# Filler products on TensorE around the first two attention units, and one copy moved from VectorE to ScalarE

## The chip, the cores and the metric

The kernel runs on one core of one Trainium2 chip. A core has a matrix engine (TensorE, PE in the profile, with its weight loads as PEld), three engines for elementwise work (VectorE or DVE, ScalarE or ACT, GpSimd or POOL), a queue that mostly issues transfers (SyncE, SP), and 16 DMA engines. The metric is the device time of one execution in microseconds; lower is better. Five runs of the kernel before gave a median of 304.19 us (303.46 to 305.06).

## The reference

Inputs q, k and v are float32 of 8 batches x 8 heads x 576 positions x 64. Attention is limited to a symmetric window of 32 positions, and a two-layer network with a sigmoid-gated activation follows on the 4608 tokens:

```python
scores = scale * np.matmul(q, k.transpose(0, 1, 3, 2))
mask = np.abs(pos[:, None] - pos[None, :]) <= window          # window = 32
scores = np.where(mask, scores, -1e9)
attn = softmax(scores)
x = (attn @ v).transpose(0, 2, 1, 3).reshape(4608, 512)
h = x @ w_in                                                  # 512 -> 2048
g = h * sigmoid(1.702 * h)
out = g @ w_out                                               # 2048 -> 512
```

## The kernel before

The 4608 tokens are cut into 36 attention units of 128 queries, each with two blocks of 64 queries and the 128 keys around each block. Two units make a tile of 256 tokens for the two layers, 18 tiles in all. The order of the instructions on each engine is the order in which the program calls them; nothing reorders it. A buffer (a tile of SBUF or a bank of PSUM) is taken from a ring of a fixed length, and the first instruction that writes it waits for the last reader or writer of what lay there before. PSUM has eight banks in four rings: two "h", one "o", four "a" and one "t" (`bank`).

The change is in `head`, the part ahead of the loop over windows. Its calls, in order, and what each puts on which engine:

- Loads. The q and k of the first 320 tokens (span "A") for four heads come by the SP and ACT queues; the rest (other heads of A, v of units 0 to 2, span "B" with the next 256 tokens, v of unit 3 and half of 4, four parts of w_in, then w_out and later spans) is issued by POOL, in that order.
- `keep_busy(n, kind)`, line 424: n products of a zero tile with itself, 128x256, into a bank of ring `kind`. Nobody reads them.
- `keys_T` and `queries_T` (lines 163 and 166): TensorE transposes keys or queries of a pair of heads into a bank; a copy on the engine given as the last argument (`cast`, line 106) moves them to kT or qT. For span B the rings are "htho" for keys and "hoth" for queries, one letter for each of the four pairs.
- `blind(u)`, line 232: two "mask products" of 128x512 that write large negative numbers into the two score banks of unit u where a key lies outside the window. The scores of units 0 to 3 are then added on top (`scores`, line 250), so that their exponentials (line 256, ACT, four for two units) need no mask afterwards.
- `odd_v(m, eng)`, lines 151 and 152: two copies of 64x528 make vo, the v of unit m moved by 64 tokens, for the second block of queries: the upper half of ve of m, and the lower half of ve of m+1.
- `values(u, kinds)`, line 279: 32 small products of the exponentials with ve and vo, into two banks of the rings named.
- `norm(u)`, lines 290 and 291: DVE takes the reciprocal of the sums and multiplies, once for each half of the heads; x results.
- `x_T(u, kind, eng)`, line 306: TensorE transposes x in two pairs, one for each half, and `eng` copies the result to xT.
- `layer1(t, d)`, line 319: a group of eight products with w_in into an "h" bank, and the activation g on ACT (line 321). ACT loads a table when it goes from exponentials to g. The third group needs the bank of the first, so it waits for the first g.

In `head`, scores of units 0 and 1 are followed by vo, values, x and transposes of unit 0, then of unit 1, then by mask products of unit 2, the transposes of span B, mask products of unit 3, scores of units 2 and 3, and then by layer 1 of the first tile with the values of units 2 and 3 in between. After that, TensorE has layer 1 and layer 2 (lines 331 and 381) to do without a break.

Of the kernel before, what the change touches and what calls it, by code (L numbers as in the profile page):

```python
# [23 lines left out]
NV = 8  # L24
# [4 lines left out]
class _Kernel:  # L29
# [117 lines left out]
    def odd_v(self, m, eng):  # L147

        vo = self.vo[m % NV]
        nxt = self.v_first if m == self.NU - 1 else self.ve[(m + 1) % NV][0:64]  # L150
        eng.tensor_copy(vo[64:128], self.ve[m % NV][64:128])
        eng.tensor_copy(vo[0:64], nxt)


    def heads_T(self, c, i, hp, kind):
# [271 lines left out]
    def head(self):  # L427

        nc, dve, act, pool = self.nc, self.nc.vector, self.nc.scalar, self.nc.gpsimd
        for hp in range(2):  # L430
            self.load_raw("k", hp, nc.sync)
            self.load_raw("q", hp, act)
        self.setup()
        for c in "kq":
            self.load_heads("A", c, (4, 8))
        self.setup_neg()
        for m in range(3):
            self.load_v(m)
        for c in "kq":
            self.load_heads("B", c)  # L440
        self.load_v(3)
        self.load_v(4, 0)
        for c in range(4):
            self.load_w_in(c)
        self.odd_v(2, pool)
        self.odd_v(3, pool)
        for c in (0, 2):
            self.load_w_out(c)
        self.setup_mask()
        self.cut_mask()  # L450
        for c in "kq":
            self.load_heads(1, c)
        self.load_w_out(1)
        self.load_v(4, 1)
        for m in range(5, 7):
            self.load_v(m)
        self.load_w_out(3)
        self.load_v(7)
        for c in "kq":
            self.load_heads(2, c)  # L460
        self.keep_busy(16)
        for hp in range(2):
            self.pair_heads("k", "A", hp, dve, self.stage["k", "raw", hp])
            self.pair_heads("q", "A", hp, act, self.stage["q", "raw", hp])
        for hp in range(4):
            self.keys_T("A", hp, "ht"[hp % 2], dve)
            self.queries_T("A", hp, "ho"[hp % 2], act)
            if hp < 2:
                self.blind(hp)
        self.scores(0)  # L470
        self.scores(1)
        self.odd_v(0, dve)
        self.keep_busy(5, "h")
        self.values(0, "hh")
        self.norm(0)
        self.odd_v(1, dve)
        self.x_T(0, "t", act)
        self.values(1, "oa")
        self.norm(1)
        self.x_T(1, "a", act)  # L480
        self.blind(2)
        for hp in range(4):
            self.keys_T("B", hp, "htho"[hp], dve)
            self.queries_T("B", hp, "hoth"[hp], act)
        self.blind(3)
        self.scores(2)
        self.scores(3)
        self.layer1(0, 0)
        self.values(2)
        self.norm(2)  # L490
        self.layer1(0, 1)
        self.values(3)
        self.norm(3)
        self.x_T(2, "t")
        self.layer1(0, 2)
        self.x_T(3, "o")
        self.layer1(0, 3)
        for d in range(4):
            self.layer1(1, d)
        dve.tensor_copy(self.v_first, self.ve[0][0:64])  # L500
        dve.tensor_copy(self.k_first, self.kT[:, :, 0:64])
        self.queries_wrap(0)
        for n in range(4):
            self.w_sums(n, 0)
        for c in "kq":
            for hp in range(4):
                self.pair_heads(c, 1, hp, dve)
        for t, d in ((0, 4), (0, 5), (1, 4), (1, 5), (0, 6), (0, 7), (1, 6), (1, 7)):
            self.layer1(t, d)
        l2 = [(lambda c=c, u=u: self.layer2(u, c, "hhot"[u], (dve, act)[u % 2])) for c in range(4) for u in range(4)]  # L510

        def run(n):
            for _ in range(n):
                l2.pop(0)()

        run(4)
        for hp in range(4):
            self.keys_T(1, hp, "a", dve)
            self.queries_T(1, hp, "a", act)
            run(1)  # L520
        self.scores(4)
        self.scores(5)
        for m in range(4, 7):
            self.odd_v(m, dve)
        self.band(4)
        run(3)
        self.band(5)
        run(1)
        self.values(4)
        self.norm(4)  # L530
        self.scores(6)
        run(1)
        self.gelu_table()
        self.values(5)
        self.norm(5)
        self.band(6)
        run(1)
        self.x_T(4, "a")
        run(1)
        self.x_T(5, "a", act)  # L540
        run(1)
        for c in "kq":
            for hp in range(4):
                self.pair_heads(c, 2, hp, pool)
        self.load_v(8)
        self.load_v(9)
        self.load_v(10)
        for c in "kq":
            self.load_heads(3, c)
        self.layer1(2, 0)  # L550
        self.values(6)
        self.norm(6)
        for n in range(2):
            self.w_sums(n, 1)
        for d in range(1, 3):
            self.layer1(2, d)
        self.x_T(6, "a")
        self.layer1(2, 3)
        for hp in range(4):
            self.keys_T(2, hp, "t", dve)  # L560
            if hp in (1, 2):
                self.w_sums(hp + 1, 1)
            self.queries_T(2, hp, "o", act)
            self.layer1(2, 4 + hp)
        for m in (7, 8, 9):
            self.odd_v(m, dve)
        for m in (11, 12, 13):
            self.load_v(m)
        for c in "kq":
            self.load_heads(4, c)  # L570
# [230 lines left out]
```

## Time and profile before

| what | value |
| --- | --- |
| median of five runs | 304.19 us (303.46 to 305.06) |
| the profiled execution's own time | 303.33 us |
| its span in the profile | 301.6 us |
| PE busy in the span | 293.6 us (97%) |
| DVE, ACT, POOL busy | 198.0, 197.0, 74.5 us |
| PE's share of the chain that ended last | 92% |
| line 319 (layer 1) PE busy | 135.2 us, 1152 products of 274 ns |
| mean granted clock of PE | 0.989 |

The span is the time from the first to the last instruction that the profile shows; what lies around it is the difference to the execution's own time. Busy shares are given for 40 equal slices of 7.54 us. PEclk is the clock that TensorE was granted, in tenths of full speed. A product's duration includes its way through the engine, so products in a row overlap, and the distance of their starts is less than the duration. The chain that ended last is followed back from the last instruction, at each step to what released it. A wait for several things is put down to the one that came last.

### The profile page before, as it was taken

Reading aid. Unit: us, or ns where it says so; the run is one execution under the profiler, and the core shown is the slowest. Engines: PE = TensorE matmul, PEld = TensorE weight load, DVE = VectorE, ACT = ScalarE, POOL = GpSimd, SP = SyncE. Lnnn points to the kernel's source line nnn. Section 1 sums busy time; section 2 is a strip of 40 time slices with the busy share of each in tenths; the row PEclk is TensorE's granted clock in tenths of the full one; section 3 lists DMA queues with packets and bytes.
Section 4 is the critical chain, followed back from the end, with each engine's and each line's share of the span. In section 5 each row is a group of like instructions: output and inputs, shape, how many; then the busy total and the mean of one; then the engine's idle time right before and its main releaser. Section 6 shows DMA issues by size and latency. Waiting matters only on the chain.

```text
span 301.6 us, 9776 instructions
## 1 busy us (share of the span) xinstructions
PE 293.6 (97%) x4165; PEld 244.1 (81%) x4165; DVE 198.0 (66%) x602; ACT 197.0 (65%) x331; POOL 74.5 (25%) x114
## 2 busy tenths in 40 slices
PE   7699999999999999999999999999999999999995
PEld 4469764866888888888888888888888888888884
DVE  3633558679795958595859585958595767684353
ACT  4576547685785858585858585859595848575330
POOL 8884516957131203320222020201000000000000
PEclk9959999999999999999999999999999999999999
DMA  9999996999999991999099909590933030303012
GB/s 145 163 206 205 197 187 117 180 181 202 195 73 160 178 136 11 161 184 138 7 163 186 141 3 141 74 139 4 139 72 107 3 108 2 104 4 104 2 70 70
DMA packets 92202, 35.16 MB, mean 117 GB/s; under 512 B 64512, under 2 KB 87808, under 8 KB 92160
## 3 DMA queue, kind: packets, MB, share of 16 engines
q0 software_dynamic: 60320, 18.16, 60.7%
q1 hardware_dynamic: 31392, 16.00, 24.2%
q8 instruction: 32, 0.52, 0.7%
q10 hardware_dynamic: 448, 0.39, 0.5%
q14 instruction: 10, 0.08, 0.1%
HBM read 36.96 MB, written 9.44 MB: 154 GB/s over the span
## 4 chain that ended last, share of the span: by engine, by line
PE 92%; DVE 4%; DMA 1%; ACT 1%; issue 0%; SPq 0%; DVEq 0%
PE h_ps L319 42%; PE o_ps L381 30%; PE o_ps L331 7%; PE pv L279 4%; PE sc L250 4%; PE tp L163 2%; DMA k_raw<-in_k_dram 1%; PE tp L689 1%; PE tp L166 1%; PE sc L232 1%; PE tp L306 1%; DVE x L291 1%; DVE p L268 0%; DVE kT L106 0%; DVE kc L106 0%; DVE o_sb L399 0%
## 5 line engine op out<-in xcount | busy, mean ns | idle before, releaser
L319 PE MATMUL h_ps<-xT,w_in_sb 128*128 128x256 bf16 x1152 | 135.2, 274 | 0.0
L321 ACT ACTIVATE g<-h_ps 128x512 f16<-128x512 f32 x144 | 85.9, 597 | 69.7 <-PE h_ps L319 67.6
L319 PEld LDWEIGHTS <-w_in_sb 128*128 128x128 bf16 x1152 | 112.4, 98 | 13.8
L144 POOL DMA_DIRECT2D ve<-in_v_dram x40 | 34.2, 860 | 122.1 <-DVE rec L290 86.5
L381 PEld LDWEIGHTS <-gs 128*128 128x128 f16 x480 | 45.8, 98 | 5.8
L381 PE MATMUL o_ps<-w_sum,gs 128*128 128x256 f16 x360 | 44.3, 273 | 0.0
L256 ACT ACTIVATE p<-sc 128x512 bf16<-128x512 f32 x72 | 37.2, 603 | 3.5 <-PE sc L250 3.4
L358 DVE TENSOR_TENSOR gs<-g 128x512 f16<-128x512 f16 x30 | 12.6, 421 | 38.7 <-ACT g L321 38.6
L381 PEld LDWEIGHTS <-g 128*128 128x128 f16 x360 | 34.2, 98 | 4.5 <-ACT g L321 0.2
L291 DVE TENSOR_TENSOR x<-pv,rec 128x256 bf16<-128x256 f32 x72 | 30.5, 424 | 2.5
L381 PE MATMUL o_ps<-w_out_sb,g 128*128 128x256 f16 x240 | 29.1, 273 | 0.0
L106 DVE COPY part<-o_ps 128x256 f32<-128x256 f32 x45 | 19.0, 423 | 12.3 <-PE o_ps L381 11.4
L399 DVE TENSOR_TENSOR o_sb<-o_ps,part 128x256 f32<-128x256 f32 x45 | 19.0, 422 | 12.1 <-PE o_ps L381 11.5
L268 DVE TENSOR_TENSOR p<-p,mask 128x512 bf16<-128x512 bf16 x64 | 24.7, 424 | 1.3 <-ACT p L256 1.1
L331 PE MATMUL o_ps<-w_out_sb,g 128*128 128x512 f16 x96 | 23.2, 380 | 0.0
L256 ACT ACT_TABLE_LOAD x15 | 19.2, 1283 | 0.3
L418 ACT ACT_TABLE_LOAD x15 | 19.2, 1283 | 0.3
L290 DVE RECIPROCAL rec<-pv 128x4 f32<-128x4 f32 x72 | 12.5, 174 | 8.2 <-PE pv L279 8.2
L106 DVE COPY kT<-tp 128x512 bf16<-128x512 bf16 (+3 forms) x24 | 12.3, 531 | 8.2 <-PE tp L163 6.1
L279 PEld LDWEIGHTS <-p 128*64 128x64 bf16 x576 | 12.0, 111 | 6.5 <-DVE p L268 1.9
L250 PEld LDWEIGHTS <-kT 64*64 64x64 bf16 x1152 | 12.0, 110 | 5.1 <-issue 4.8
L279 PE MATMUL pv<-ve,p 128*64 128x65 bf16 x288 | 15.7, 198 | 0.4 <-DVE p L268 0.3
(71 smaller groups left out, 287.0 us busy)
## 6 DMA issues: line engine op xcount, KB each, us to landing
out_dram<-o_sb SPq DMA_DIRECT2D x34, 256.0 KB, 2.8
ve<-in_v_dram POOLq DMA_DIRECT2D x32, 128.0 KB, 5.0
w_in_sb<-in_moe_w_in_dram POOLq DMA_DIRECT2D x4, 512.0 KB, 11.2
w_out_sb<-in_moe_w_out_dram POOLq DMA_DIRECT2D x4, 512.0 KB, 12.2
ks<-in_k_dram POOLq DMA_DIRECT2D x2, 448.0 KB, 10.3
qs<-in_q_dram POOLq DMA_DIRECT2D x2, 448.0 KB, 12.7
ks<-in_k_dram POOLq DMA_DIRECT2D x3, 256.0 KB, 7.7
qs<-in_q_dram POOLq DMA_DIRECT2D x3, 256.0 KB, 8.4
```

The lines of the kernel that those rows point to most:

```text
L106: (eng.copy if eng is self.nc.scalar else eng.tensor_copy)(out, in_)
L144: self.nc.gpsimd.dma_start(self.ve[m % NV][off:off + n, :, :self.D], self.v[b, :, s:s + n, :].rearrange("h s d -> s h d"))
L250: nc.tensor.matmul(sc[eo][lo:lo + 64, 2 * hp + blk, :], self.kT[r, hp, at:at + 64], self.qT[r, JT * hp:JT * hp + JT, q0:q0 + 16], start=(s ...
L256: nc.scalar.activation(p[:, eo].rearrange("k h (s j) -> k h s j", j=JT), sc[eo].rearrange("k h (j s) -> k h s j", j=JT), AF.Exp, scale=sel ...
L268: self.nc.vector.tensor_mul(pv, pv, msk.to_broadcast([128, 4, 2, SQ]))
L279: nc.tensor.matmul(acc[half][blk * 64:blk * 64 + 64, hh, :], p[:, h % 2, h // 2 * 2 + blk, :], vt[:, h, :D + 1], start=(hh == 0), stop=(hh ...
L291: nc.vector.tensor_mul(x[:, hs, :], acc[half][:, :, :D], rec[:, hs, :].to_broadcast([128, 4, D]))
L319: nc.tensor.matmul(hps[:, i, :], self.w_in_sb[:, kr, ff * 128:(ff + 1) * 128], self.xT[t][:, kr, :], start=(i == 0 and kr == 0), stop=(i = ...
L321: nc.scalar.activation(self.g[t][:, ffs[0]:ffs[1] + 1:ffs[1] - ffs[0], :], hps, AF.Gelu_apprx_sigmoid)
L331: nc.tensor.matmul(o_ps, self.g[t][:, ff, s * 128:(s + 1) * 128], self.w_out_sb[:, ff, :], start=(ff == 0), stop=(ff == self.NFF - 1))
L381: nc.tensor.matmul(self.part[t, key], x, y, start=(first and k == 0), stop=(k == 7), skip_group_check=True)
L418: self.nc.scalar.activation(self.spark, self.spark, AF.Gelu_apprx_sigmoid)
```

## The change

In `odd_v` the two copies go through `cast`, which takes ScalarE's copy or another engine's, so that ScalarE can be given the work. In `head`:

- the vo copies of unit 1 go from DVE, where they came after the norm of unit 0, to ACT, where they come after the exponentials of units 0 and 1;
- six unread products into "o" come after the values of unit 0, two more into "o" after the transposes of x of unit 0, eight into "a" after the values of unit 1, and two into "h" ahead of the transposes of span B;
- the mask products of unit 3 come right after those of unit 2, before the transposes of span B instead of after them.

On TensorE these are 18 more products; no load or store is added or moved.

```diff
-        eng.tensor_copy(vo[64:128], self.ve[m % NV][64:128])
-        eng.tensor_copy(vo[0:64], nxt)
+        self.cast(eng, vo[64:128], self.ve[m % NV][64:128])
+        self.cast(eng, vo[0:64], nxt)
...
         self.odd_v(0, dve)
+        self.odd_v(1, act)
         self.keep_busy(5, "h")
         self.values(0, "hh")
         self.norm(0)
-        self.odd_v(1, dve)
+        self.keep_busy(6, "o")
         self.x_T(0, "t", act)
+        self.keep_busy(2, "o")
         self.values(1, "oa")
         self.norm(1)
+        self.keep_busy(8, "a")
         self.x_T(1, "a", act)
         self.blind(2)
+        self.blind(3)
+        self.keep_busy(2, "h")
         for hp in range(4):
             self.keys_T("B", hp, "htho"[hp], dve)
             self.queries_T("B", hp, "hoth"[hp], act)
-        self.blind(3)
         self.scores(2)
         self.scores(3)
```

## The prediction

> **What bounds the kernel now.** I began with the busy shares in 40 slices:
>
> ```profile
> PE   7699999999999999999999999999999999999995
> PEclk9959999999999999999999999999999999999999
> ```
>
> TensorE (PE) is full from slice 4 on, so the end comes earlier only if dense work begins earlier. One stretch is odd: in the third slice (15.1 to 22.6 us) PE had half its clock. I located it with windows of 0.1 us (edges at 15.10 and 21.92) and cut the stage at these edges; the columns are PE, weight loads, DVE, ACT, POOL, clock, DMA share and GB/s:
>
> ```profile
> 8.27:11.69 3.42, 2.39 (x84) 1.59 (x73) 2.60 (x8) 2.40 (x6) 3.42 (x6) 1.00 1.65 152
> 11.69:15.10 3.41, 2.11 (x34) 1.08 (x36) 1.87 (x7) 1.17 (x2) 2.01 (x3) 1.00 1.73 181
> 15.10:18.51 3.41, 3.32 (x100) 2.33 (x102) 1.64 (x4) 1.49 (x4) 2.71 (x5) 0.50 1.25 206
> 18.51:21.92 3.41, 3.41 (x67) 2.37 (x58) 0.64 (x3) 3.26 (x5) 3.06 (x12) 0.50 1.24 207
> ```
>
> The half clock follows PE's emptiest stretch. Next, the chain that ended last, within these stages (start, us, what):
>
> ```profile
> 12.05 0.38 DVE vo L152
> 12.43 0.04 issue
> 12.47 0.31 PE pv L279 x7
> ...
> 13.56 0.43 DVE x L291
> ...
> 15.06 0.65 PE tp L166 x16
> ...
> 16.20 0.85 PE tp L166 x15
> 17.05 0.97 PE sc L232 x2
> 18.02 1.00 PE sc L250 x41
> 19.02 1.82 PE h_ps L319 x8
> 20.84 0.58 PE pv L279 x12
> 21.42 1.24 PE h_ps L319 x8
> 22.66 0.38 PE pv L279 x16
> 23.04 0.33 PE tp L306 x4
> 23.37 0.87 PE h_ps L319 x8
> ```
>
> Up to 14 us the chain goes through DVE; from 16.2 it is PE alone, slow: eight products of line 319 take 1.82 us at 19.02 and 0.87 at 23.37. At 15.06 PE also waited for a transfer, in the waits of this stage:
>
> ```profile
> PEld L166 <- DMA qs<-in_q_dram: 0.2, 1, 0.2
> ```
>
> Last, ACT close behind PE in the timeline:
>
> ```profile
> 18.64 2.07 ACT L256 ACTIVATE p<-sc 128x512 bf16<-128x512 f32 x4 [1.18 <-PE sc L250]
> 20.73 1.28 ACT L321 ACT_TABLE_LOAD   x1
> 22.02 1.28 ACT L321 ACTIVATE g<-h_ps 128x512 f16<-128x512 f32 x2
> ```
>
> Its first g ends at 22.62 and frees the bank that the third layer-1 group needs; that group ran at 23.37. So ACT has 0.7 us in hand: a faster PE gains 0.7 us here and then meets ACT, unless the exponentials begin earlier too.
>
> **What the Trainium skill says.** "TensorE: Matmul & The Clock Gate", "What's actually happening": after an idle window of some 3.4 us TensorE gets half its clock, a busy window gives it back, and the windows run freely of the kernel's start. The trace agrees: 15.10 to 21.92 is 6.82 us, two such windows. The same page, "Part 4: PE-mode transpose", says that transposes do not count as busy for this in the same way. The trace speaks for it: in 15.10:18.51 PE was busy 3.32 of 3.41 us, 1.86 of it line 166's transposes, and the clock stayed at half. "ScalarE: Activation LUTs", "What ACT_TABLE_LOAD costs", gives 1283 ns for the load; the trace has the same.
>
> **The change part by part.** Sums are against the profiled execution, 303.33 us (span 301.6, 1.73 around it), assuming full clock throughout; then I ask whether it holds.
>
> Price of an unread product: line 424's five take 0.72 us with a mean of 275 ns each, so their starts are (0.72-0.275)/4 = 0.11 apart.
>
> 1. Six after the values of unit 0: 6 x 0.11 = 0.66, from 10.34 to 11.00. PE waited for x until 11.12 there, so they are hidden.
>
> 2. Two after the first transposes of x: 11.78 to 12.00. The values of unit 1 use the same bank and so wait for the end of the second, 11.89 + 0.275 = 12.17. Before they waited for DVE's vo until 12.47; hidden.
>
> 3. Both vo copies of unit 1 leave DVE (0.38 each, ended 12.43) for ACT, free from 11.02, when its exponentials end. No row shows such a copy on ACT: between 0.45 (one of its two 128x256 copies took 0.40) and 0.65 (POOL took 0.64); I take 0.6, by ACT's 128x512 copy of 0.59. They end at 12.25: 0.18 us earlier. The low price gives 11.95, but then step 2's 12.17 decides; the high one 12.35. Behind them on ACT waits the first xT copy, at 11.99 before and now 12.3 to 12.9. Its reader, line 319, comes at 18.5 or later.
>
> 4. Values at 12.29 instead of 12.47. From them to the end of the second x was 13.99-12.47 = 1.52, so 13.81. The eight products run from about 12.55 to 13.43. They delay the first pair of transposes (x ready at 13.27) by 0.15, but not the second: 13.86 instead of 14.04.
>
> 5. Mask products of unit 2: 13.98 to 14.41. Those of unit 3 now come here. The first runs at 14.41. The second reuses the bank of the transposed x, so it needs ACT's copy of it, which began 0.33 after the second pair: 14.19 + 0.59 = 14.78. That is a new wait, 0.2 us, with the whole of PE's queue behind it. It runs 14.82 to 15.04, then two junk products to 15.26. The transposes of line 166 begin there, against 14.69 for keys and 15.06 for queries: 0.2 us later than the transfer would allow.
>
> 6. 64 transposes at full clock: about 0.15 per eight (7.34 to 7.79 has three such steps), paced by four DVE copies of 0.42 and four ACT copies of 0.40, because banks are reused. Keys' last copy ends at 17.44, queries' at 17.68; before 17.30 and 17.46. So 0.22 later.
>
> 7. The mask products of unit 3, 0.97 on the chain at half clock, are gone from between transposes and scores. In the A stage the exponential began 0.36 after the last qT copy (8.61 to 8.97). So it begins at 17.68 + 0.36 = 18.04, not 18.64: 0.60 earlier.
>
> 8. ACT: 18.04 + 2.07 + 0.02 + 1.28 + 0.01 + 0.60 = 22.02. PE: w_in's first transfer, issued at 10.03, takes 8.5 (shortest of the four), so the first layer-1 group runs 18.57 to 19.44, values to 19.82, the second group to 20.69; unit 3's exponentials end at 20.11, so values to 21.07, transposes to 21.40. Then PE waits for ACT's bank: the third group starts at 22.06 instead of 23.37.
>
> The gain is 1.3 us. It stays, because PE is full afterwards. The next limits: qs of span 1 lands before DVE's 36.70, its first copy ends at 36.99, PE reads it at 39.35, 2.3 in hand. The last v of that stage, issued at 34.87 and 9.9 on its way, lands at 44.8; DVE used it at 45.80, so up to 0.3 us moves into DVE's queue, ahead of masks whose values have over 1 us in hand. At 303.33 this is 302.0; at the median, 304.19, it is **302.9**.
>
> Does the clock hold? In 11.69:15.10 a full array is given eight junk products after the values, two at their start, and two more mask products, about 1.3 us on top of 2.11, all in gaps: it should hold at 15.10. The next window is weaker: 0.22 of junk, 0.7 of scores, and transposes. If these count little, it is no fuller than the window that lost the clock.
>
> **The rivals.**
>
> *The clock falls at 18.51 instead.* For it: the half clock survived 15.10:18.51 although PE was busy. Against it: 4.86:8.27, also mostly transposes and masks, kept the clock. Then PE has 18.57 to 20.35, values to 20.95, the second group to 22.4 (full clock again at 21.92), values and transposes to 23.05: the third group 0.32 earlier, 303.9. If the clock falls at 15.10 after all, so that the change doesn't do what it says, removing the masks from before the scores leaves about 0.4: 303.8. One answer.
>
> *The median has less to give.* The windows run freely, and this profile may have caught a dear position. With the half clock ending 1 us earlier in before, the second group runs at full clock and the third would start near 22.9: gain 0.7 to 0.8, 303.45.
>
> *Slower.* The clock falls at 18.51 and stays low for two windows, to 25.3. Both groups then cost 1.8, the third begins at 23.6 and takes 1.75 to 25.35, against 24.24: 1.1 us lost, 305.3. It decides once the half clock lasts beyond about 24. Against it: at half clock, the same groups brought the clock back at 21.92.
>
> **How the numbers follow.** Full clock throughout 0.58 (302.9, own range 302.3 to 303.3); falls all the same 0.20 (303.8 to 303.9); less to give 0.15 (303.45); slower 0.07 (305.3). About 0.3%, 0.9 us, is what a measurement of this kernel can tell from none; 303.28 is the bound. Faster 0.58, the two middle cases within 0.3%: 0.35, slower 0.07. ACT's price moves the sum by 0.1 either way, the clock's position in before by 0.6 downward, so the range is 302.2 to 304.1.
>
> **What would show it.** Right: clock 1.00 from 15 to 25 us; vo of unit 1 on ACT ending near 12.25; the second mask product of unit 3 waiting for ACT near 14.8; the first exponential of unit 2 near 18.0; the third layer-1 group near 22.1, waiting for ACT. Wrong: a 0.50 in any slice there, the line-166 transposes beginning after 15.6, or a new wait in 34 to 46 us.

## The result

The changed kernel takes 304.11 us at the median (28 executions, 303.25 to 307.52), the kernel before 304.19 (47 executions). The ratio, which weighs all executions and not the medians alone, is 1.0015, 95% interval 0.9999 to 1.003: no change that can be told from none. Forecast were 302.9 us and a gain; the median lies 0.01 us beyond the upper end of the range, 304.1. The profiled execution took 303.66 us (span 302.0).

The executions are of two kinds. Each lists the mean clock that TensorE was granted. In 14 of 28 it was 0.998 or more, and their median is 303.58 us; in the other 14 it was 0.984 to 0.995, and their median is 305.20. The kernel before, in the comparisons below, had 0.983 to 0.989 in nearly every execution, which is two or three windows of half clock (two of 3.41 us each lower the mean over the span by 0.011).

The profiled execution is of the first kind. Its busy shares, as shown of before:

```profile
PE   8869999999999999999999999999999999999995
PEclk9999999999999999999999999999999999999999
```

The half clock is gone. The same stretches of time as before (PE, weight loads, DVE, ACT, POOL, clock, DMA share and GB/s) show what came in its place:

```profile
8.27:11.69 3.42, 2.89 (x93) 2.11 (x81) 1.76 (x7) 3.05 (x7) 3.42 (x5) 1.00 1.65 143
11.69:15.10 3.41, 3.03 (x37) 1.98 (x36) 1.46 (x5) 1.80 (x4) 2.23 (x4) 1.00 1.73 173
15.10:18.51 3.41, 3.09 (x133) 2.15 (x131) 1.60 (x4) 1.63 (x6) 2.27 (x4) 1.00 1.25 206
18.51:21.92 3.41, 1.46 (x24) 1.07 (x24) 0.61 (x2) 3.38 (x6) 3.06 (x12) 1.00 1.25 208
```

In 11.69:15.10 PE is 3.03 us busy instead of 2.11, as meant. But in 18.51:21.92, where it had been busy throughout at half clock, it works 1.46 us and stands idle for the rest. The chain that ended last has this idle time, called the stand from here on, as one piece (start, us, what):

```profile
15.20 0.38 PE sc L232
...
15.80 0.26 PE tp L166 x8
...
19.55 0.37 PE pv L279 x15
19.92 1.95 issue
21.87 0.22 PE pv L279
22.09 0.98 PE h_ps L319 x8
...
23.77 0.87 PE h_ps L319 x8
```

PE does 15 of the 16 value products of unit 2, stands 1.95 us, and does the last. "Issue" means that it waited for nothing that the profile shows; the last product needs no tile that the 15 before it did not need. The third layer-1 group starts at 23.77 on this chain; before it was 23.37, and the forecast was 22.06. The span is longer by the same 0.4 us.

Two theories of the stand. **F:** PE was waiting for its own instructions. They come over the DMA engines in packets of 16 KB: section 3 of the page of before lists 32 "instruction" packets, 0.52 MB, on queue 8, against 8330 products and weight loads on PE in section 1, so some 260 instructions to a packet. "Runtime: NRT & Kernel Launch", section "Instruction fetch mechanics", of the Trainium skill says the same: refills in 16 KiB blocks of 256 instructions, the next one fetched while the current one is executed, at a cost that is "mostly hidden". Counting PE's records in the trace, the stand is ahead of number 705. PE passed number 449, 256 earlier, at 16.10 us. Then, by the DMA view in parts:

```profile
q0 software_dynamic: 941, 0.89, 125.6%
```

for 15 to 19.3 us (packets, MB, and the time that the packets took as a share of the 16 engines' time; packets overlap, so it can pass 100%): the kernel's own loads alone, and from 19.3 to 20.4

```profile
q0 software_dynamic: 221, 0.22, 118.7%
q8 instruction: 1, 0.02, 5.1%
```

So the packet waited some 3.3 us to start. It was over by 20.4, and PE went on at 21.87, 5.77 us after it had entered the block: there is a third part, of 1.5 us or somewhat more, between the packet's end and the next instruction. PE had used up the block in 3.8 us. Before, at half clock, the block took it 6.5 us (16.3 to 22.8), and the fetch was hidden behind that. **H:** the last product waits for data or a bank by a semaphore that the profile does not name.

### The profile page after: what moved, and what is told of

Its sections match the earlier page's. It is cut to its first block, busy times and chain, and to the rows that moved or that the text cites. A ratio compares the mean times of both kernels' runs of the same rounds, so it can differ in the third digit from the quotient of the medians.

```text
span 302.0 us, 9815 instructions
## 1 busy us (share of the span) xinstructions
PE 293.8 (97%) x4183; PEld 244.8 (81%) x4183; DVE 196.6 (65%) x600; ACT 198.0 (66%) x333; POOL 74.4 (25%) x114
## 4 chain that ended last, share of the span: by engine, by line
PE 91%; DVE 4%; DMA 1%; issue 1%; POOL 1%; ACT 0%; POOLq 0%; DVEq 0%
PE h_ps L319 41%; PE o_ps L381 30%; PE o_ps L331 7%; PE pv L279 4%; PE sc L250 4%; PE tp L163 2%; DMA ve<-in_v_dram 1%; PE tp L693 1%; PE tp L306 1%; DVE x L291 1%; DVE p L268 0%; DVE kT L106 0%; DVE o_sb L399 0%; POOL neg L224 0%; DVE part L106 0%
## 5 line engine op out<-in xcount | busy, mean ns | idle before, releaser
L106 DVE COPY vo<-ve 64x528 bf16<-64x528 bf16 x65 | 19.7, 303 | 2.7 <-DMA ve<-in_v_dram 1.2
L279 PE MATMUL pv<-vo,p 128*64 128x65 bf16 x288 | 15.3, 197 | 2.4 <-issue 1.9
```

What stands on the lines that cost most here:

```text
L106: (eng.copy if eng is self.nc.scalar else eng.tensor_copy)(out, in_)
L279: nc.tensor.matmul(acc[half][blk * 64:blk * 64 + 64, hh, :], p[:, h % 2, h // 2 * 2 + blk, :], vt[:, h, :D + 1], start=(hh == 0), stop=(hh ...
```

## The experiments

Every ratio is to the kernel before on the same chip.

**Where the stand is.** The first kernel (e1) puts 16 more pairs of weight load and product ahead of everything, with the same columns in all; the second (e2) 48 more.

```diff
-        self.keep_busy(16)
+        self.keep_busy(32, cols=128)           # e1
+        self.keep_busy(64, rows=64, cols=64)   # e2
```

> The changed kernel, with the 16 unread products of 256 columns at the very start cut into 32 of 128 columns: the same columns, 32 more PE instructions ahead of everything. Theory F (PE's instructions come in blocks of 256 over the DMA engines; PE used up a block at the last value product of unit 2 and stood until the next had come): the stand moves 32 instructions earlier in the program, to the last product of the first layer-1 group (line 319), from about 19.2 to 21.5 us, and lasts about 2.2 us; the last value product of unit 2 no longer waits. Theory H (that product waits for data or a bank, by a semaphore that the profile doesn't name): the stand stays at that product and ends near 21.9. Both: time within 0.4 us of the changed kernel.

> The changed kernel, with the 16 unread products at the start made 64 of 64 columns on 64 rows of output: 96 more PE instructions ahead of everything. Theory F: a block now ends in the scores of unit 3, near 18.1 us. PE entered that block near 12.8, so with 5.8 us for a fetch (16.10 to 21.87 in the changed kernel) the next is there near 18.6: a stand of 0.6 us at most, ahead of exponentials that are due at 19.3. The third layer-1 group then starts near 22.1 instead of 23.6, and the profiled time is about 302.2, 1.5 us under the changed kernel's. Theory H: the stand of 1.9 us stays at the last value product of unit 2, and the time is the changed kernel's. A third possibility: the smaller products don't bring the clock up at 5 to 7 us, and all is later by 1 us or more.

The chain of the first kernel:

```profile
20.38 0.87 PE h_ps L319 x7
21.25 1.77 issue
23.02 0.37 PE h_ps L319
```

The chain of the second:

```profile
18.44 0.52 issue
18.96 0.53 PE sc L250 x25
```

The stand has moved by exactly the pairs added, so it is in all three kernels ahead of the same number, 705, of PE's records. In e1 it is ahead of the eighth layer-1 product: that one and the 15 value products are 16. In e2 it is ahead of the last 25 scores: 25, 8 and 15 are 48. Theory H has fallen. The stand in e2 is 0.52 us, as expected; in e1 it is 1.77 us, 0.4 less than expected. The third group of e2 came at 23.85, not 22.1, and in this execution the clock fell at 19.02, as in the other case of the prediction. The window ahead of that, in e2:

```profile
15.61:19.02 3.41, 2.64 (x113) 1.90 (x114) 1.60 (x4) 1.89 (x6) 3.29 (x6) 1.00 1.24 207
```

PE was busy 77% of the window that lost the clock; it held transposes and scores, and the stand of 0.52 us as well.

In e1 the clock fell too, after the stand. Windows of e1:

```profile
19.60:23.01 3.41, 1.63 (x55) 1.24 (x55) 0.10 (x1) 3.05 (x6) 3.06 (x12) 1.00 1.24 207
23.01:26.42 3.41, 3.40 (x43) 2.18 (x43) 1.30 (x5) 1.68 (x3) 2.36 (x4) 0.50 1.24 206
```

The stand empties a window, and the next one has half clock, now in dense layer 1, where each of these 3.4 us gives half the work: 1.7 us lost, as an estimate. (This execution had also lost the clock from 12.77 to 16.18, after a window with PE busy 1.68 us.) Two other kernels below, h1 and g2, show the same in their profiles. In h1:

```profile
18.91:22.33 3.42, 1.79 (x34) 1.27 (x34) 1.21 (x4) 2.76 (x5) 3.08 (x12) 1.00 1.23 203
22.33:25.74 3.41, 3.41 (x35) 2.72 (x34) 1.70 (x6) 1.17 (x2) 2.36 (x4) 0.50 1.24 208
```

Why then did the changed kernel's profile keep the clock, with a stand of 1.95 us? Its windows lie elsewhere. Its clock falls only at 303.81, behind the end. Before has the same fall at 301.82, which is 82 steps of 3.413 us after the edge at 21.92. Counted back in such steps from 303.81, the changed kernel's windows are these, not the ones from 15.10 and 18.51:

```profile
13.68:17.09 3.41, 3.16 (x67) 1.91 (x66) 1.41 (x5) 1.23 (x3) 1.15 (x3) 1.00 1.51 193
17.09:20.50 3.41, 2.70 (x110) 1.98 (x103) 1.28 (x4) 2.90 (x7) 3.23 (x7) 1.00 1.24 207
20.50:23.92 3.42, 2.05 (x32) 1.66 (x33) 1.13 (x5) 2.29 (x3) 3.20 (x11) 1.00 1.25 206
```

The stand, 19.92 to 21.87, falls on both sides of the edge at 20.50, and neither window lost the clock. In e1, h1 and g2 it lies within one window. So in these four profiles the clock was lost where the stand lay within one window and kept where an edge divided it. PE's busy time alone doesn't decide it: 2.05 us kept the clock here and 2.64 us lost it in e2. The 2.05 hold layer 1's full products and the 2.64 mostly small ones, which fits the prediction's reading that transposes count little; no run here separates transposes from other small products.

The medians are 305.78 (ratio 1.0041, 1.0017 to 1.0064) for e1, which was expected within 0.4 us of the changed kernel's 304.11 and isn't, and 303.68 (0.9992, 0.9969 to 1.0016) for e2. In e2 the 5 executions of clock 0.998 or more have a median of 302.66 and the 9 others 304.45. So with full clock and no long stand the forecast time was there, but seldom.

**Why the fetch takes so long.** Two kernels use the identity instead of the first layer's weights in line 319 (that layer is left out of the computation). One (g2, the control) keeps all transfers. The other (g1, the quiet kernel) has no w_in transfers and issues the first w_out later, so that the DMA engines are idle when PE asks for its block.

```diff
-        for c in range(4):
-            self.load_w_in(c)
...
-        for c in (0, 2):
-            self.load_w_out(c)
         self.setup_mask()
         self.cut_mask()
+        for c in (0, 2):
+            self.load_w_out(c)
```

> The changed kernel with the first layer's weights replaced by the identity tile in every product of line 319 (so that layer is left out of the computation), all transfers kept: the control for the next. Theory F: PE stands 1 to 2.5 us on instructions in the values of unit 2 or within a few instructions of them, as in the changed kernel, and the packet with the next instructions starts 2 us or more after PE entered the block.

> The same, without the four transfers of w_in, and with the first two of w_out issued after the mask is set up instead of before: the DMA engines have little to do from about 16 to 20 us, when PE asks for its next block. If the fetch is slow because it queues among the kernel's own transfers: its packet starts within about 1 us of PE's entry into the block, and PE stands less than 0.6 us there, where the control stands 1 to 2.5. If a fetch takes 5.8 us by itself: the stand is that of the control.

The chain of the control:

```profile
20.34 0.37 PE pv L279 x15
20.71 2.04 issue
```

PE entered the block at 17.07, and the packet started after 20.3. In the quiet kernel PE entered at 15.82; the DMA view shows nothing from 16 to 16.6 and this from 16.6 to 17.8:

```profile
q8 instruction: 1, 0.02, 5.0%
```

It started 0.9 us after PE's entry instead of over 3 us, and there is no stand. PE used up this block in 3.5 us. As an estimate, 0.9 to start, 1.0 for the packet (5.0% of 16 engines for 1.2 us) and the 1.5 behind it make 3.4: even with idle DMA engines the fetch was hidden only just. The quiet kernel's chain:

```profile
17.96 2.05 ACT p L256 x4
...
21.33 0.60 ACT g L321
...
21.98 1.03 PE h_ps L319 x8
```

So the start of the fetch is held up by the kernel's own loads. "DMA: Bandwidth & Descriptors", section "Queues, rings and completion order", of the Trainium skill says that an engine goes round its queues packet by packet; that fits a packet that waits for what is already under way, but these runs don't show how the turns are taken. Without the stand the chain runs through ACT, with exponentials at 17.96 (forecast 18.04) and the third group at 21.98 (forecast 22.06).

**The parts alone.** First vo of unit 1 on ACT and nothing else (e3); then that and the moved mask products, without the 18 products added (e4).

```diff
         self.odd_v(0, dve)
+        self.odd_v(1, act)
...
-        self.odd_v(1, dve)
```

> The kernel before with the vo copies of unit 1 on ACT and nothing else of the change. Theory F and the clock: TensorE still gets half clock from about 15 to 22 us, no stand on instructions, the values of unit 1 start about 0.2 us earlier, and the time is that of before within 0.3 us. Rival (the copies on ACT are what costs the changed kernel its gain): slower than before by 0.5 us or more, with a later xT or qT copy.

> The changed kernel without its 18 added unread products: vo of unit 1 on ACT and the mask products of unit 3 moved forward. Theory F and the clock: half clock for two windows again, PE takes longer than 5.8 us for the block of instructions in question and doesn't stand, and with the masks gone from before the scores the time is 0.2 to 0.6 us under that of before. Rival (the moved mask products' wait for ACT is what costs): line-166 transposes begin 0.4 us or more later than before and the time is above that of before.

The first: 303.45 us, ratio 0.9982 (0.9969 to 0.9995), a small gain, of some 0.55 us where at most 0.3 was expected; the copies on ACT are not the trouble. Where the gain comes from isn't shown: in e3's profile the values of unit 1 came at 12.52, no earlier than before. The second: 304.01, ratio 0.9986 (0.997 to 1.0003), which can't be told from none. Neither stood on instructions, and every execution of both had half clock (0.983 to 0.994), as expected. In the second's chain line 166 began at 16.23, 1.5 us later than before (14.76), behind four mask products that took 1.71 us at half clock. The rival had that right, but not the time.

**Holding the clock.** One kernel (f3) adds to the changed one a repeat of a mask product of unit 3 (same values, same bank) after each pair of span B's transposes; two (f1, f2) add this to e2, with 8 instead of 5 unread products ahead of the values of unit 0, and f2 has part of its filler in smaller pieces.

```diff
             self.queries_T("B", hp, "hoth"[hp], act)
+            self.blind_again(3, hp % 2)
```

> The changed kernel with the same four repeated mask products and nothing else. Theory F: the stand on instructions stays, 1.5 to 2 us in the values of unit 2 or at the end of the layer-1 group before them, because its place depends on the number of instructions alone; fastest runs about 303.3 as in the changed kernel, and still some at 305 or above, because the stand itself empties a window. Rival (the clock alone cost the changed kernel its gain): fastest runs near 302.2 and the median under 303.2.

> The kernel of the 64 small products at the start, with the mask products of unit 3 written again (same values, same bank) after each of the four pairs of span B's transposes, four of 512 columns in all, and 8 instead of 5 unread products ahead of the values of unit 0. Theory F and the clock (transposes hardly count for the clock, so a window that holds them needs full products): half clock falls near 19 us in fewer executions than in that kernel, where 9 of 14 had it; median 302.6 to 303.0. A block of instructions ends at the first scores of unit 3, near 18 us, with a stand of 0.6 us at most. Rival (the added products delay the transposes more than the clock gives): the median is that of the kernel without them, 303.7, or above.

> The previous kernel with 14 of the filler products cut in two, which puts 28 more PE instructions ahead of the block's end: it falls in the scores of unit 2, which wait for the last copy of queries anyway, and PE enters the block before 12 us. Theory F: no stand above 0.2 us, time that of the previous kernel or up to 0.4 us less. Rival (the instructions are not what it waited for): nothing changes, or the filler in smaller pieces runs slower and costs 0.3 us or more.

The chain of f3, whose stand has moved by the four pairs added, from the 16th to the 12th value product:

```profile
20.62 0.31 PE pv L285 x11
20.93 1.09 issue
22.02 0.28 PE pv L285 x5
```

All 12 of its executions had a clock of 0.998 or more: 303.41 to 304.11, median 303.77 (ratio 0.9995, 0.9984 to 1.0006). Some at 305 or above had been expected, and there were none. The clock can thus be held against transposes with full products, but these four lie on the way (the chain has each as a piece of 0.32 us), and the stand stays, at 1.09 us. For f1 and f2 the medians were 303.66 (0.9997, 0.9979 to 1.0015) and 303.94 (1.0007, 0.9988 to 1.0025), the clock held in 13 and 11 of 14, and stands of 0.39 and 0.24 us. Expected of f1 was up to 303.0: the rival was right, holding the clock in this way costs as much as it wins. The smaller filler of f2 won nothing.

Then fewer repeats on top of e2's start and the 8 products: three (f4), after the second and third pair and ahead of the last quarter of unit 2's scores; or two (f5), without the third pair's.

> 64 small products at the start, 8 ahead of the values of unit 0, and three repeated mask products of unit 3 where PE waits: after the second and third pair of span B's transposes, and ahead of the last quarter of unit 2's scores. Theory F and the clock: no stand over 0.6 us, the clock holds in most executions, and with 0.4 us less of added products on the way than with four the third layer-1 group starts near 22.3; median 302.7 to 303.3, below before. Rival (what is won by the clock is always paid by the products that hold it): median 303.6 or above.

> The same with two repeated mask products: after the second pair and ahead of the last quarter of unit 2's scores. Theory F and the clock: where the clock holds, 302.1 to 303.2 as with none; it is lost in some executions, fewer than 9 of 14; median between 302.5 and 303.4. Rival: as with none, half of the executions at half clock near 19 us, median near 303.7.

Three: 303.73 (0.9993, 0.9972 to 1.0014), not the 302.7 to 303.3 expected. Two: 303.23, ratio 0.997 (0.9951 to 0.9989), the clock held in 11 of 13 executions, as expected. It beats the kernel before by 0.3%. In its chain ACT's first g is over at 22.64 and the third group starts at 22.68.

**The moved mask products.** The changed kernel with the masks of unit 3 back behind span B's transposes (h1), and the same (i1) with e2's start and 8 unread products, not 5, ahead of the values of unit 0.

```diff
         self.blind(2)
-        self.blind(3)
...
             self.queries_T("B", hp, "hoth"[hp], act)
+        self.blind(3)
```

> The changed kernel with the mask products of unit 3 back where they were, after span B's transposes; the filler products and vo on ACT stay. Theory F and the clock: the two mask products (0.4 us at full clock) sit on the way to the scores, but they fill the window of the transposes, so fewer executions lose the clock near 18.5; the stand on instructions stays, 1 to 2 us, and with it losses one window later. Median 303.5 to 304.3, not faster than before by more than 0.3%. Rival (the move of the masks is what costs): median under 303.2.

> Masks of unit 3 back after span B's transposes, as in the last run, with the 64 small products at the start and 8 ahead of the values of unit 0 (102 more PE instructions ahead of the block's end). If the moved masks cost because they held up PE's entry into the block (15.40 us in the last run, 16.10 in the changed kernel) and because they left the window of the transposes empty: no stand of over 0.9 us and none after 19 us, since the block now ends in the scores of unit 3 and is asked for before 13 us; the clock holds in most executions; the third layer-1 group starts near 22; median 302.4 to 302.9, below before and below the last run by 0.3 to 0.7. If the stand was not what was left of the cost there: the median stays near the last run's 303.1.

The first: 303.12, ratio 0.9984 (0.997 to 0.9999); the clock held in 17 of 20 executions, with a median of 303.05, although its profile, of an execution that lost the clock, has a stand of 1.63 us. I had expected 303.5 or more and the rival was right: where the masks stood in the change cost about 1 us at the median (304.11, on another chip). Two things go with it. In the profile PE entered the block at 15.40 instead of 16.10, so the stand ended at 21.07 instead of 21.87 (5.67 and 5.77 after entry); 0.1 us of this lies ahead of the masks, since the second transposes of x came at 14.13 instead of 14.24. And the clock was lost in 3 of 20 executions instead of 14 of 28. The second: 303.22 (0.9983, 0.9967 to 1.0), not the 302.4 to 302.9 expected. Its stand is 0.5 us, and where the clock held (16 of 22) the median is 302.83, but it lost the clock in 6 of 22. In its profile vo of unit 0 waited 2.3 us for v, so that the third group came at 22.77 in spite of everything. Whether the masks' place costs something beyond entry and window stays open.

| kernel | executions with a clock of 0.998 or more | their median, us | executions below | their median, us |
| --- | --- | --- | --- | --- |
| changed | 14 | 303.58 | 14 | 305.20 |
| e1, 32 instructions more | 6 | 303.67 | 11 | 306.18 |
| e2, 96 more | 5 | 302.66 | 9 | 304.45 |
| f1, four masks and e2's start | 13 | 303.57 | 1 | 306.15 |
| f2, the same, smaller filler | 11 | 303.84 | 3 | 305.75 |
| f3, four masks | 12 | 303.77 | 0 | |
| f4, three masks and e2's start | 12 | 303.45 | 4 | 305.37 |
| f5, two masks and e2's start | 11 | 303.02 | 2 | 304.92 |
| h1, masks back | 17 | 303.05 | 3 | 304.77 |
| i1, masks back and e2's start | 16 | 302.83 | 6 | 304.48 |

## Why the prediction was wrong

Steps 1 to 7 held, 0.2 to 0.5 us late in this execution because v of unit 1 landed later (vo of unit 0 waited 1.2 us for it, not at all before). The six and the eight products were hidden. The two were not quite: the values of unit 1 waited for them until 12.60, while ACT's vo was there at 12.39, because the transposes of x ahead of them were late. The vo copies on ACT took 0.64 us each, forecast 0.6 with bounds 0.45 and 0.65. The values came at 12.64, forecast 12.29; the second mask product waited for ACT's copy of x until 15.20, forecast 14.82; the exponentials began at 18.23, forecast 18.04; and ACT's first g was over at 22.21, forecast 22.02.

**Step 8 failed.** It let PE run from the first layer-1 group to the third, bounded by w_in, the exponentials and ACT's bank. PE stood 1.95 us for instructions ahead of the last value product, so the second group came at 22.09 instead of 19.82. The list of what could be late next held banks and transfers of data, not PE's own instructions. The page of before had their packets in section 3, and the 6.5 us for one block in the trace; the sum let PE run through these 256 instructions, which took 3.8 us in the event, without asking where the next would come from. In the quiet kernel, without the stand, the third group came within 0.1 us of the rest of the sum.

**The check of the clock was half right.** It took the windows' edges, 15.10 and 18.51, from one execution of before, although it said itself that the windows run freely; in the changed kernel's profile they lie at 17.09 and 20.50. It was right that the filler fills the stretch ahead of the transposes and that the transposes themselves are weak: e2's profile shows the clock lost behind them with PE 77% busy. That case was priced at 303.8 to 303.9 with a chance of 0.20. Half the executions had a lower clock, at 305.20. The price was probably too small because a window emptied by the stand puts the half clock after 22 us, into dense work: e1 shows it at 23.01, h1 at 22.33. Where the lower clock lay in the changed kernel's own other executions isn't seen, since the trace is of one that held it.

The rival of lesser gain from another window position is not what happened: before had half clock in nearly all executions, so there was enough to win. The slower rival's mechanism, half clock past 24 us, is what e1 had, at 307.31 us in an execution with a second window of half clock ahead of it; it was priced at 305.3, for one cause alone. Not foreseen was that the two kinds of execution cancel: 303.58 lies 0.6 under before's median and 305.20 1.0 above it. That the median of all came out within 0.1 us of before is this balance, not a change without effect.

## What to carry to other kernels

Before a stretch of many small instructions is made faster, count them: 256 instructions on PE should take longer than their fetch, which was 5.1 to 6.6 us here while the loads ran. The block's end can be moved by adding or removing instructions far ahead, and a stand that moves with the count is a fetch. Filler for the clock counts as instructions as well, and filler on the way costs what it wins, as f1 and f3 show. Take the edges of the clock's windows from each profile anew, not from another execution.

## What the runs showed of the hardware

- PE's next packet of 256 instructions starts within 1 us when the DMA engines are quiet (0.9 us in g1), and some 3 us after it is asked for among loads at some 205 GB/s (3.3 us in the changed kernel, over 3.2 in g2). It takes 0.9 to 1.0 us, and PE goes on about 1.5 us after its end. From PE's entry into a block to its first instruction of the next: 5.8, 5.3, 6.0, 5.7 and 5.1 us in the changed kernel, e1, e2, h1 and f3, and 6.6 in f1.
- The stand was ahead of PE's record number 705 in every profile that had one, whatever the instruction there.
- With four full products added among the transposes, the clock held in 13 of 14 executions of f1 and 12 of 12 of f3, against 5 of 14 of e2 and 14 of 28 of the changed kernel. A window with PE busy 2.64 of 3.41 us, mostly in small products, lost the clock in e2; one with 2.05 us, layer 1's full products among them, kept it in the changed kernel.
- A stand of 1.6 to 2.0 us within one window was followed by a window of half clock in the profiles of e1, h1 and g2; divided between two windows, one of 1.95 us was not, in the changed kernel.
- The loads of the head land at different times from execution to execution: the last q of span B at 15.0 us before, 16.18 in e3 and 16.78 in g2, by the chains and waits of their profiles, though none of these kernels issues it differently. That is as much as the whole change was to bring, and it limits what a single profile can tell.
